# The head of an FNet-gated kernel: one chain of statistics, chunk 0 by pass, sums ahead of the second chunk's split, and the next operands written into the order

## The chip, the cores and the metric

The kernel runs on one core of a Trainium2 chip. The metric is device time in microseconds (us) of one execution, and the program has to fit one launch. Engines are named as in the profile: PE is TensorE (matmul), PEld its weight loads, DVE is VectorE, ACT is ScalarE, POOL is GpSimd, SP is SyncE, which issues most DMAs. "SPq" is SP's instruction queue.

## The reference, cut to what matters

Input x is [1, 2048, 512] in float32. The seq matrices are 2048 x 2048, the hidden ones 512 x 512, the layer between has 1792 units.

```python
xn = (x - mean(x)) / sqrt(var(x) + 1e-5)              # per row
a, b = xn @ dft_hid_re.T, xn @ dft_hid_im.T
s = dft_seq_re @ a - dft_seq_im @ b                   # real part of a 2-D DFT
h = relu(xn @ w1 + b1) ** 2
g = silu(h @ w2 + b2)
out = x + s * g
```

## The kernel before, in words

Every product in float32 is made of three matmuls: an operand is split into a high part (a copy rounded to the matmul's own format, written by ACT, `split_hi`, L70) and a low part (the remainder, a subtraction on DVE, `split_lo`, L73), and `PASSES` (L34) lists the three pairs high-high, high-low, low-high. The sequence transform comes first: chunks of 256 output rows (`c`, eight of them) by tiles of 2 x 128 input rows (`j`, eight of them). Chunks 0 and 1 are plain products; chunks 2 to 7 use a Strassen-like form with seven products (`mm`, L300, `PRODUCTS`, L50) on operands that `moving` (L217) makes: three sums on DVE (`sums_b`), then the splits into `g0` and `g1`. Then `stage2` (L282) multiplies a chunk's result, split into high and low parts (`pq`, L276, `pq_parts`, L169), with the hidden matrices (24 matmuls to a half, into one PSUM bank), ACT copies the bank to `ysb` (L295) and SP stores it to DRAM (`y`, L297). The layer with w1 and w2 and the gating follow; the change doesn't touch them.

The first part, L364 to L445, is a manual schedule: every engine's queue gets the instructions in the order in which the code writes them.

- *Start.* SP loads x and the constants `r` (of `ct`), tile 0 in halves: x one, r one, x two, r two. `WARM` (L21) gives 8 matmuls in bfloat16 and 5 in the other format on zeros. Tile 0 goes by halves: statistics (`ln_stats`, bn_stats and bn_aggr), root on ACT (`ln_root`), four small DVE operations (`ln_rstd`), `ln_xn`, splits, twelve matmuls, then the same for the second half.
- *Chunk 0.* For each tile `products` (L350) makes 24 matmuls of 128 x 512, two halves of twelve. By pass (tiles 0 to 3) all four blocks `k` go through high-high, then high-low, then low-high. Otherwise (tiles 4 to 7) each block makes its three matmuls in a row. The statistics of the next tile stand between the splits of this one.
- *Chunk 1.* Tile j's products need the constants' split of tile j, which `split(*plain_parts(1, j + 1))` (L434) makes one tile ahead into two buffers (`g1a`, `g1b`), so that it waits until the products of tile j - 1 are done. Beside the products, DVE and ACT work through a list `aside` (L426): the sums over xn (`sums`, L157) and their splits (`split_sums`, L179) for the operands of chunks 2 to 7, the splits of chunk 0's result (`pq_parts`), the hidden matrix's load and split (`wd_split`, L259). The loop takes items until their costs reach `ASIDE` = 4.2. `split_s1` (L184) follows one tile behind. `stage2(0, 0)` stands behind tile 6 and `stage2(0, 1)` behind tile 7.
- *Behind it.* `split_s1(7)`, `pq_parts(1)`. Then, outside the manual schedule, `prep()` (L649), which keeps up to three constant tiles loading and makes the operand of the next step, is called twice (L656) and once in each step of the loop at L659. There a scheduler places the instructions: it may put them ahead of what the manual schedule wrote last, on each engine's queue. The matmuls of that loop are issued after `plain_end`, the last matmul of `stage2(0, 1)`.

Tile pools tie the parts together: `r` has three buffers, `g1a` and `g1b` are those of the plain splits too, and `t` is shared by the sums over xn and by `moving`.

Of the kernel before, what the change touches and what calls it, by code (L numbers as in the profile page):

```python
# [16 lines left out]
NJ, NP = NS // 2, NF // 2  # L17
CW = 256
NC = S // CW
TC = 512  # L20
NTC = S // TC  # L21
WARM = 8, 5
PLAIN = 2

ASIDE = 4.2
# [8 lines left out]
PASSES = ((HI, HI), (HI, LO), (LO, HI))  # L34
# [30 lines left out]
def fnet_gated_kernel(ctx, tc, x, xt, ct, wd, w1, w2, b1, b2, out):  # L65
# [4 lines left out]
    def split_hi(hi, lo, src):  # L70
        nc.scalar.activation(hi, src, AF.Copy)  # L71

    def split_lo(hi, lo, src):  # L73
        return nc.vector.tensor_tensor(lo, src, hi.bitcast(F32), op=ALU.subtract)  # L74
# [37 lines left out]
    def load_x(j, hs=slice(0, 2)):  # L112

        if j not in xr:
            xr[j] = buf(f"pq{j // 2 % 2}{j % 2}", [P, 2, D], f"x{j}")
        nc.sync.dma_start(xr[j][:, hs], x.rearrange("(h j p) d -> j p h d", h=2, p=P)[j][:, hs])

    def ln_stats(j, hs=slice(0, 2)):
        t = xr[j]
        sm = buf("bn", [P, 12], f"bn{j}_{hs.start}", bufs=3)  # L120
        for h in range(hs.start, hs.stop):
            bn = sm[:, 6 * h:6 * h + 6]
            nc.vector.bn_stats(bn, t[:, h])
            nc.vector.bn_aggr(stats[:, :, h, j], bn)
# [3 lines left out]
    def ln_root(j, hs=slice(0, 2)):  # L128
        n = hs.stop - hs.start
        t = root[j] = buf("sm", [P, 4], f"root{j}_{hs.start}", bufs=3)  # L130
        nc.scalar.activation(t[:, 0:n], stats[:, 1, hs, j], AF.Sqrt, bias=eps)

    def ln_rstd(j, hs=slice(0, 2)):
        n = hs.stop - hs.start
        y, q = root[j][:, 0:n], root[j][:, 2:2 + n]
        var = rstd = stats[:, 1, hs, j]
        nc.vector.reciprocal(y, y)

        nc.vector.scalar_tensor_tensor(q, var, EPS, y, op0=ALU.add, op1=ALU.mult)
        nc.vector.scalar_tensor_tensor(q, q, -0.5, y, op0=ALU.mult, op1=ALU.mult)  # L140
        nc.vector.scalar_tensor_tensor(rstd, q, 1.5, y, op0=ALU.add, op1=ALU.mult)
# [9 lines left out]
    def xc_parts(j, h):  # L151
        s = slice(2 * h, 2 * h + 2)
        return XC[j][:, s, HI, :], XC[j][:, s, LO, :], halves(xn32[j][:, h])
# [30 lines left out]
    def split_s1(j):  # L184
        split(XC[j][:, S1, HI, :], XC[j][:, S1, LO, :], s1[j // ND][:, j % ND])
        return 0.4

    raw, part = {}, {}

    def load_c(c, j, hs=slice(0, 2)):  # L190
        if (c, j) not in raw:
            raw[c, j] = buf("r", [P, 4, CW], f"r{c}_{j}", bufs=3)
        q = slice(2 * hs.start, 2 * hs.stop)
        nc.sync.dma_start(raw[c, j][:, q], ct[c, j, :, q])

    def plain_parts(c, j, hs=slice(0, 2)):
        if (c, j) not in part:
            part[c, j] = buf("g1" + "ab"[j % 2], [P, 2, 4, CW], f"g{c}_{j}", F32R)
        g, r = part[c, j], raw[c, j]
        s = slice(2 * hs.start, 2 * hs.stop)  # L200
        return g[:, HI, s], g[:, LO, s], r[:, s]
# [15 lines left out]
    def moving(key, r):  # L217

        k = "ab"[turn[0] % 2]
        turn[0] += 1  # L220
        g0 = buf(f"g0{k}", [P, 2, 3, CW], f"g0_{key}", F32R)
        g1 = buf(f"g1{k}", [P, 2, 4, CW], f"g1_{key}", F32R)
        t = buf("t", [P, 4, CW], f"t_{key}", bufs=2)
        sums_b(t, r)
        split(g0[:, HI], g0[:, LO], r[:, I11:I21 + 1])
        split(g1[:, HI], g1[:, LO], t)
        return g0, g1
# [114 lines left out]
    def plain_banks(c):  # L342
        if c == 0:
            two_, b_, c_ = (bank(tag, f"pq0_{tag}") for tag in ("b2", "bb", "bc"))
            accs[c] = [two_[:, 0], two_[:, 1], b_[:, 0], c_[:, 0]]
        else:
            three_, a_ = (bank(tag, f"pq1_{tag}") for tag in ("b3", "ba"))
            accs[c] = [three_[:, 0], three_[:, 1], three_[:, 2], a_[:, 0]]

    def products(c, j, h, by_pass=False):  # L350

        g = part[c, j]
        for passes in [[q] for q in PASSES] if by_pass else [PASSES]:
            for k in range(ND):
                for a_, b_ in passes:
                    w = XC[j][:, 2 * h + k // 2, a_, k % 2 * P:(k % 2 + 1) * P]
                    nc.tensor.matmul(accs[c][k], w, g[:, b_, 2 * h:2 * h + 2],  # L357
                                     start=j == 0 and h == 0 and (a_, b_) == (HI, HI),
                                     stop=j == NJ - 1 and h == 1 and (a_, b_) == (LO, HI))

    one, two = slice(0, 1), slice(1, 2)
    order = [(c, j) for c in range(PLAIN) for j in range(NJ)]

    with tc.manual_schedule(engines=None):  # L364
        nc.scalar.activation(stats[:, 1, 0, 0:1], eps, AF.Sqrt)
        for hs in (one, two):
            load_x(0, hs)
            load_c(0, 0, hs)
        for j in range(1, 3):
            load_x(j)  # L370
            load_c(0, j)
        load_x(3)

        warm = bank("b3", "warm")[:, 0]
        for n, (count, dtype) in enumerate(zip(WARM, (mybir.dt.bfloat16, F32R))):
            zeros = buf("g0" + "ab"[n], [P, 512], f"zeros{n}", dtype)
            nc.vector.memset(zeros if n == 0 else zeros.bitcast(F32), 0.0)
            for _ in range(count):
                nc.tensor.matmul(warm, zeros[:, 0:P], zeros, start=True, stop=True)
        plain_banks(0)  # L380
        ln_stats(0, one)
        ln_root(0, one)
        for h, hs in enumerate((one, two)):
            g = plain_parts(0, 0, hs)
            split_hi(*g)
            ln_rstd(0, hs)
            ln_xn(0, h)
            split_hi(*xc_parts(0, h))
            if h == 0:
                ln_stats(0, two)  # L390
                ln_root(0, two)
            split_lo(*g)
            if h == 1:
                ln_stats(1)
                g = plain_parts(0, 1)
                split_hi(*g)
                ln_root(1)
            split_lo(*xc_parts(0, h))
            products(0, 0, h, True)
        load_c(0, 3)  # L400
        load_x(4)
        for j in range(1, NJ):
            ln_rstd(j)
            for h in range(2):
                ln_xn(j, h)
                split_hi(*xc_parts(j, h))
            split_lo(*g)
            load_c(*order[j + 3])
            if j + 4 < NJ:
                load_x(j + 4)  # L410
            split_lo(*xc_parts(j, 0))
            if j + 1 < NJ:
                ln_stats(j + 1)
                ln_root(j + 1)
            split_lo(*xc_parts(j, 1))
            for h in range(2):
                products(0, j, h, j < 4)
            g = plain_parts(*order[j + 1])
            split_hi(*g)
            if j == 2:  # L420
                nc.sync.dma_start(b1s, b1)
                nc.sync.dma_start(b2s, bcast(b2, D))
        split_lo(*g)


        aside = chain(sums(0), (split_sums(j) for j in range(ND)), pq_parts(0), wd_split(0),  # L426
                      sums(1), (split_sums(j) for j in range(ND, NJ)), wd_split(1))
        plain_banks(1)
        for j in range(NJ):
            n = NJ + j  # L430
            if n + 3 < len(order):
                load_c(*order[n + 3])
            if j + 1 < NJ:
                split(*plain_parts(1, j + 1))  # L434
            for h in range(2):
                products(1, j, h)
            spent = 0
            if j:
                spent = split_s1(j - 1)
            while spent < ASIDE:  # L440
                spent += next(aside, ASIDE)
            if j > NJ - 3:
                plain_end = stage2(0, j - NJ + 2)
        split_s1(NJ - 1)
        list(pq_parts(1))  # L445
    raw.clear()


    W1, W2, H, fin = {}, {}, {}, {}
# [188 lines left out]
    def plus(c, e, k, cols=slice(0, 2)):  # L638
# [1 line left out]
        z = e[:, k, w]  # L640
        nc.vector.tensor_tensor(z, z, fin[c][2 + k // 2][:, k % 2, w], op=ALU.add)
        nc.sync.dma_start(at(out[c * TC:(c + 1) * TC], k)[:, cols], z.rearrange("p (k e) -> p k e", e=256))

    steps = [(c, j) for c in range(PLAIN, NC) for j in range(NJ)]
    AHEAD = 2
    todo = list(steps)
    loads = list(steps)

    def prep():  # L649
        while loads and len(raw) < 3:  # L650
            load_c(*loads.pop(0))
        if todo:
            s = todo.pop(0)
            part[s] = moving(f"{s[0]}_{s[1]}", raw.pop(s))

    for j in range(AHEAD):  # L656
        prep()

    for c, j in steps:  # L659
        if j == 0:  # L660
            ms = banks(c)
        g = part.pop((c, j))
# [261 lines left out]
```

## Time and profile before

| what | us |
|---|---|
| median of the runs (717.65 to 718.12) | 717.79 |
| the profiled execution's own time | 717.76 |
| its span, first to last instruction | 716.0 |
| TensorE busy | 706.6 |
| first product of chunk 0, tile 0 | 7.16 |
| first product of chunk 0, tile 1 | 14.45 |
| first product of chunk 1 | 55.10 |
| first matmul of stage2(0, 1) | 106.39 |
| first product of chunk 2 | 111.99 |

A row of the timeline has the start, the duration, the engine, the line and operation, what is written and read, how many were merged, and in brackets how long the engine stood idle before it and what ended that. A row of the windows has, for a stretch of the span, each engine's busy time and count, then the granted TensorE clock, the DMA share and GB/s. Matmuls are pipelined: a row's duration has the drain in it, so that the step from one start to the next is what a matmul costs. Times are from the span's start.

### The profile page before, as it was taken

What the parts mean: (1) busy time and instruction counts of PE and PEld (TensorE: products, weight loads), DVE (VectorE), ACT (ScalarE), POOL (GpSimd) and SP (SyncE); (2) the same over time, 40 slices, a digit from 0 to 9 for tenths busy, and PEclk for the clock granted to TensorE, in tenths of its full rate; (3) what the DMA queues carried; (4) which work ended last, traced back from release to release, by engine and by line L of the source; (5) the groups of instructions that cost most, each with busy time, mean ns of one, the idle gap of its engine ahead of it and who ended that gap; (6) DMA issues with size and microseconds to landing.
All of it is one profiled execution on the core that took longest, in us unless ns stands there. A gap on an engine that the chain in (4) does not pass through costs nothing.

```text
span 716.0 us, 12693 instructions
## 1 busy us (share of the span) xinstructions
PE 706.6 (99%) x5149; PEld 665.4 (93%) x5149; DVE 585.2 (82%) x887; ACT 348.2 (49%) x475; POOL 5.2 (1%) x8
## 2 busy tenths in 40 slices
PE   8999999999999999999999999999999999999996
PEld 5778778999999999999998999999999999999996
DVE  7987964679599697797796864999988989989897
ACT  4434533444453444544443423767767774444451
POOL 0000000000000000000000000000000000101000
PEclk9999999999999999999999999999999999999999
DMA  8524340623563553743833678975733996676644
GB/s 287 198 102 162 121 162 16 221 99 138 194 219 133 206 192 133 255 172 120 289 122 113 230 276 295 355 282 195 269 120 148 350 406 215 187 224 163 221 143 152
DMA packets 55018, 141.09 MB, mean 197 GB/s; under 512 B 5040, under 2 KB 21680, under 8 KB 53680
## 3 DMA queue, kind: packets, MB, share of 16 engines
q1 hardware_dynamic: 49840, 124.56, 50.0%
q10 hardware_dynamic: 4032, 14.68, 5.2%
q0 software_dynamic: 1088, 1.05, 1.0%
q8 instruction: 40, 0.66, 0.4%
q14 instruction: 18, 0.15, 0.1%
HBM read 97.00 MB, written 43.27 MB: 196 GB/s over the span
## 4 chain that ended last, share of the span: by engine, by line
PE 92%; DVE 5%; DMA 1%; issue 1%; ACT 0%; DVEq 0%; SPq 0%
PE m_b L304 24%; PE yps L289 13%; PE m_b_o L591 10%; PE hps L537 10%; PE hps_b L537 6%; PE m_bb L304 5%; PE m_ba L304 5%; PE pq_b L357 5%; PE m L591 3%; PE hps_ba L537 3%; PE m_bb_o L591 2%; PE m_ba_o L591 1%; PE m_bc_o L591 1%; PE hps_bb L537 1%; DVE g L74 1%; PE pq_ba L357 1%
## 5 line engine op out<-in xcount | busy, mean ns | idle before, releaser
L304 PE MATMUL m_b<-g,xc 128*128 128x256 f32 x1440 | 181.3, 281 | 0.0
L304 PEld LDWEIGHTS m_b<-g,xc 128*128 128x128 f32 x1440 | 175.5, 189 | 0.4
L74 DVE TENSOR_TENSOR g<-r,g 128x768 fp32r<-128x768 f32 (+2 forms) x65 | 65.5, 1008 | 54.8 <-ACT g L71 54.8
L71 ACT ACTIVATE g<-r 128x768 fp32r<-128x768 f32 (+2 forms) x65 | 57.7, 888 | 95.5 <-PE m_b L304 52.2
L289 PE MATMUL yps<-wd,pq 128*128 128x512 f32 x384 | 93.8, 395 | 0.0
L289 PEld LDWEIGHTS yps<-wd,pq 128*128 128x128 f32 x384 | 70.4, 188 | 15.3
L591 PE MATMUL m_b_o<-w,g 128*128 128x256 f32 x588 | 75.2, 283 | 0.0
L591 PEld LDWEIGHTS m_b_o<-w,g 128*128 128x128 f32 x588 | 72.3, 191 | 0.1
L357 PE MATMUL pq_b<-g,xc 128*128 128x512 f32 x240 | 65.3, 400 | 2.5 <-ACT xc L71 1.3
L74 DVE TENSOR_TENSOR g<-t,g 128x1024 fp32r<-128x1024 f32 x48 | 58.7, 1222 | 8.8 <-ACT g L71 8.7
L537 PE MATMUL hps<-xT,w 128*128 128x256 f32 x504 | 61.9, 282 | 0.0
L537 PEld LDWEIGHTS hps<-xT,w 128*128 128x128 f32 x504 | 60.9, 190 | 0.1
L357 PEld LDWEIGHTS pq_b<-g,xc 128*128 128x128 f32 x240 | 44.0, 188 | 16.7 <-ACT xc L71 3.3
L71 ACT ACTIVATE g<-t 128x1024 fp32r<-128x1024 f32 x48 | 50.3, 1048 | 14.4 <-PE m_ba L304 6.8
L548 ACT ACTIVATE h<-h,b1s 128x512 f32<-128x512 f32 x56 | 37.4, 716 | 17.6 <-DVE h L254 17.6
L71 ACT ACTIVATE g<-hr 128x768 fp32r<-128x768 f32 (+1 forms) x28 | 35.5, 1266 | 21.1 <-DVE hr L213 5.3
L74 DVE TENSOR_TENSOR g<-hr,g 128x768 fp32r<-128x768 f32 (+1 forms) x28 | 41.6, 1485 | 2.3 <-ACT g L71 2.2
L304 PE MATMUL m_bb<-g,xc 128*128 128x256 f32 x288 | 43.3, 283 | 0.0
L304 PE MATMUL m_ba<-g,xc 128*128 128x256 f32 x288 | 42.9, 281 | 0.0
L304 PEld LDWEIGHTS m_bb<-g,xc 128*128 128x128 f32 x288 | 39.3, 189 | 1.8
L304 PEld LDWEIGHTS m_ba<-g,xc 128*128 128x128 f32 x288 | 38.0, 189 | 0.0
L537 PE MATMUL hps_b<-xT,w 128*128 128x256 f32 x288 | 36.2, 282 | 0.0
(167 smaller groups left out, 1018.7 us busy)
## 6 DMA issues: line engine op xcount, KB each, us to landing
r<-in_ct SPq DMA_DIRECT2D x63, 512.0 KB, 3.6
hd<-h ACTq DMA_DIRECT2D x28, 512.0 KB, 4.2
hr<-hd SPq DMA_DIRECT2D x28, 512.0 KB, 4.2
w1d<-w0g SPq DMA_DIRECT2D x21, 512.0 KB, 3.2
w<-w1d SPq DMA_DIRECT2D x6, 1792.0 KB, 9.7
w<-w2d SPq DMA_DIRECT2D x4, 1792.0 KB, 9.9
y<-ysb SPq DMA_DIRECT2D x16, 256.0 KB, 3.1
fin<-y SPq DMA_DIRECT2D x16, 256.0 KB, 5.1
```

The lines of the kernel that those rows point to most:

```text
L71: nc.scalar.activation(hi, src, AF.Copy)
L74: return nc.vector.tensor_tensor(lo, src, hi.bitcast(F32), op=ALU.subtract)
L289: ins = nc.tensor.matmul(ps, PQ[c, m, k // 2][:, a_, w:w + P], WD[m, k][:, b_, :], start=n == 0, stop=n == 2 * ND * 3 - 1)
L304: nc.tensor.matmul(ps[:, d * CW:(d + 1) * CW], w[:, a_, d * P:(d + 1) * P], mv(b_), start=first and d == 0 and (a_, b_) == (HI, HI), stop= ...
L357: nc.tensor.matmul(accs[c][k], w, g[:, b_, 2 * h:2 * h + 2], start=j == 0 and h == 0 and (a_, b_) == (HI, HI), stop=j == NJ - 1 and h == 1 ...
L537: nc.tensor.matmul(product(ms, k), W1[p][a][:, a_, q * P:(q + 1) * P], xT[c, q][:, b_, b], start=share not in first, stop=q == 1 and (a_, ...
L548: nc.scalar.activation(x_[:, s], x_[:, s], AF.Relu, bias=b1s[:, f:f + 1])
L591: nc.tensor.matmul(m[:, k * 256:(k + 1) * 256], g[:, a_, a, k * P:(k + 1) * P], W2[p][:, b_, b], start=p == 0 and k == 0 and (a_, b_) == ( ...
```

## The change

- `WARM` gets 8 instead of 5 of the second kind of warm-up matmul.
- SP loads both halves of x's tile 0 before both halves of the constants.
- Tile 0 has one chain of statistics for both halves (operations on 128 x 2 instead of twice 128 x 1). On DVE both `ln_xn` come next, then the low parts of both constant halves, the low part of xn's first half, the statistics of tile 1, the low part of the second half. Both halves' matmuls follow.
- All of chunk 0 goes by pass, tiles 4 to 7 too.
- `beside(0)` takes from `aside` once before chunk 1's loop, so that the four sums over xn stand ahead of the split of (1, 1), and each later item one tile earlier.
- `prep()` is moved into the manual schedule: the first call stands behind the loop of chunk 1 and so behind `stage2(0, 1)` with its copy and its store, the second behind `pq_parts(1)`. Its loads stand where it is called.

```diff
-WARM = 8, 5
+WARM = 8, 8
...
-        for passes in [[q] for q in PASSES] if by_pass else [PASSES]:
+        for passes in [PASSES] if c else [[q] for q in PASSES]:
...
+    def prep():
+        while loads and len(raw) < 3:
+            load_c(*loads.pop(0))
+        if todo:
+            s = todo.pop(0)
+            part[s] = moving(f"{s[0]}_{s[1]}", raw.pop(s))
...
         for hs in (one, two):
             load_x(0, hs)
+        for hs in (one, two):
             load_c(0, 0, hs)
...
-        ln_stats(0, one)
-        ln_root(0, one)
+        ln_stats(0)
+        ln_root(0)
+        split_hi(*plain_parts(0, 0, one))
+        ln_rstd(0)
         for h, hs in enumerate((one, two)):
-            g = plain_parts(0, 0, hs)
-            split_hi(*g)
-            ln_rstd(0, hs)
             ln_xn(0, h)
             split_hi(*xc_parts(0, h))
             if h == 0:
-                ln_stats(0, two)
-                ln_root(0, two)
-            split_lo(*g)
-            if h == 1:
-                ln_stats(1)
-                g = plain_parts(0, 1)
-                split_hi(*g)
-                ln_root(1)
-            split_lo(*xc_parts(0, h))
-            products(0, 0, h, True)
+                split_hi(*plain_parts(0, 0, two))
+        for hs in (one, two):
+            split_lo(*plain_parts(0, 0, hs))
+        split_lo(*xc_parts(0, 0))
+        ln_stats(1)
+        g = plain_parts(0, 1)
+        split_hi(*g)
+        ln_root(1)
+        split_lo(*xc_parts(0, 1))
+        for h in range(2):
+            products(0, 0, h)
...
+        def beside(spent):
+            while spent < ASIDE:
+                spent += next(aside, ASIDE)
+
+        beside(0)
         for j in range(NJ):
...
-            spent = 0
-            if j:
-                spent = split_s1(j - 1)
-            while spent < ASIDE:
-                spent += next(aside, ASIDE)
+            beside(split_s1(j - 1) if j else 0)
             if j > NJ - 3:
                 plain_end = stage2(0, j - NJ + 2)
+        raw.clear()
+        prep()
         split_s1(NJ - 1)
         list(pq_parts(1))
-    raw.clear()
+        prep()
...
-    for j in range(AHEAD):
-        prep()
```

More of the change, by code (lines that the diff above doesn't have):

```diff
@@ L348, in plain_banks, with products @@
             accs[c] = [three_[:, 0], three_[:, 1], three_[:, 2], a_[:, 0]]
-    def products(c, j, h, by_pass=False):
+    def products(c, j, h):
         g = part[c, j]
-        for passes in [[q] for q in PASSES] if by_pass else [PASSES]:
+        for passes in [PASSES] if c else [[q] for q in PASSES]:
             for k in range(ND):
@@ L362, in fnet_gated_kernel @@
     order = [(c, j) for c in range(PLAIN) for j in range(NJ)]
+    steps = [(c, j) for c in range(PLAIN, NC) for j in range(NJ)]
+    todo = list(steps)
+    loads = list(steps)
+    def prep():
[4 more added lines that the diff above has]
+            part[s] = moving(f"{s[0]}_{s[1]}", raw.pop(s))
     with tc.manual_schedule(engines=None):
@@ L416, in fnet_gated_kernel @@
             for h in range(2):
-                products(0, j, h, j < 4)
+                products(0, j, h)
             g = plain_parts(*order[j + 1])
@@ L642, in plus @@
         nc.sync.dma_start(at(out[c * TC:(c + 1) * TC], k)[:, cols], z.rearrange("p (k e) -> p k e", e=256))
[L644 to L654, printed above, removed]
-    for j in range(AHEAD):
-        prep()
     for c, j in steps:
```

## The prediction, made before the changed kernel ran

> **What bounds the kernel now.** Read first the chain of waits and the DMA issues on the page, then the windows that cut the span at the chunks, then the timeline engine by engine where a window shows idle TensorE.
>
> ```profile
> PE 92%; DVE 5%; DMA 1%; issue 1%; ACT 0%; DVEq 0%; SPq 0%
> ...
> r<-in_ct SPq DMA_DIRECT2D x63, 512.0 KB, 3.6
> ```
>
> ```profile
> 106.40:424.00 317.60, 317.60 (x2374) 303.29 (x2373) 245.24 (x363) 136.46 (x186) 0.00 (x0) 1.00 0.50 174
> 424.00:710.00 286.00, 285.99 (x2355) 283.60 (x2354) 248.82 (x347) 163.17 (x209) 4.99 (x4) 1.00 0.67 233
> ```
>
> From 106.4 to 710 us TensorE (first busy figure of each window) has no idle time. So the end is the start of that dense stretch plus a fixed amount of matmul work: what the change does before 106.4 moves the end one for one, and a hole opened at the head of the dense stretch does so too. The change touches only that part; past the first tiles of chunk 2 the built program of the changed kernel has the same instructions in the same order.
>
> **Part 1, start and chunk 0.**
>
> ```profile
> 3.77 0.69 DVE L123 BATCH_NORM_STATS2 bn<-x 128x6 f32<-128x512 f32 x1 [2.06 <-DMA x<-in_x]
> 4.57 0.18 DVE L124 BATCH_NORM_AGGREGATE stats<-bn 128x2 f32<-128x6 f32 x1
> ...
> 6.48 0.63 ACT L71 ACTIVATE xc<-xn 128x512 fp32r<-128x512 f32 x1 [0.87 <-DVE xn L148]
> ...
> 7.16 0.73 PE L357 MATMUL pq_b<-g,xc 128*128 128x512 f32 x2 [0.40 <-ACT xc L71]
> ...
> 8.05 0.64 ACT L71 ACTIVATE g<-r 128x512 fp32r<-128x512 f32 x1 [0.46 <-DMA r<-in_ct]
> ...
> 10.21 0.69 DVE L123 BATCH_NORM_STATS2 bn<-x 128x6 f32<-128x512 f32 x1
> ...
> 11.83 0.66 DVE L74 TENSOR_TENSOR xc<-xn,xc 128x512 fp32r<-128x512 f32 x1
> ...
> 12.40 0.16 DVE L137 RECIPROCAL root<-root 128x2 f32<-128x2 f32 x1
> ...
> 14.45 0.74 PE L357 MATMUL pq_b<-g,xc 128*128 128x512 f32 x2 [0.73 <-ACT xc L71]
> ```
>
> One chain of statistics for both halves puts a second pair of bn_stats and bn_aggr (0.8 us, the step from 3.77 to 4.57) ahead of the first root: first product at 7.95 instead of 7.16. The second half of x, now second on SP, has 0.9 us behind the first for its 256 KB; were it late, the first product would be, but tile 1's chain hangs on a later landing: the second constant half lands fourth in either order (8.03), ScalarE has it split at 8.69, then come on VectorE its low part, the low part of xn and the two statistics of tile 1: 8.72 + 0.6 + 0.6 gives 9.91 for bn_stats instead of 10.21. The 1.62 us from there to the low part at 11.83 and the 2.62 us to the product at 14.45 stay. Tile 1 starts 0.30 us earlier, at 14.15. Four small operations and a root that go stood beside that landing and bring nothing. Bounds: no gain, or 0.8 if that half lands earlier; I take 0.3. The three added warm-up matmuls end before 7.95, as the clock is full from about 6.4; at worst they cost 0.1.
>
> ```profile
> 31.42 0.43 PE L357 MATMUL pq_b<-g,xc 128*128 128x512 f32 x1
> 32.27 1.81 PE L357 MATMUL pq_b<-g,xc 128*128 128x512 f32 x5 [0.42 <-DVE g L74]
> ...
> 55.10 2.26 PE L357 MATMUL pq_b<-g,xc 128*128 128x512 f32 x9
> ```
>
> ```profile
> 46.20 0.16 DVE L137 RECIPROCAL root<-root 128x2 f32<-128x2 f32 x1
> ```
>
> By pass in tiles 4 to 7: a product takes 0.233 us (24 in 5.6 us). At tile 4 the second product needs the low part of the constants, so it starts 0.85 us after the first instead of 0.23, and five take 1.81 us instead of 1.33. With a 0.1 at tile 7 that makes 1.2 us. By pass the low part is needed after four products, 0.93 us in, and tile 4's release (32.27) came 0.85 in: just in time. VectorE sets the pace from there: the reciprocals of tiles 1 and 7, at 12.40 and 46.20, are six tiles of 5.63 us apart against TensorE's 5.60, which takes 0.05 back. So chunk 1 begins at 55.10 - 0.30 - 1.15 = 53.65.
>
> **Part 2, chunk 1.** The four sums over xn now come before the second constant tile's split.
>
> ```profile
> 50.72 1.23 DVE L74 TENSOR_TENSOR g<-r,g 128x1024 fp32r<-128x1024 f32 x1 [0.30 <-ACT g L71]
> 56.40 1.23 DVE L74 TENSOR_TENSOR g<-r,g 128x1024 fp32r<-128x1024 f32 x1 [4.45 <-ACT g L71]
> 57.54 1.22 DVE L166 TENSOR_TENSOR s<-xn 128x1024 f32<-128x1024 f32 x1
> ...
> 88.44 1.22 DVE L74 TENSOR_TENSOR g<-r,g 128x1024 fp32r<-128x1024 f32 x1
> ```
>
> ```profile
> 88.70 0.39 PE L357 MATMUL pq_b<-g,xc 128*128 128x512 f32 x1
> 89.71 2.13 PE L357 MATMUL pq_b<-g,xc 128*128 128x512 f32 x8 [0.62 <-DVE g L74]
> ```
>
> Before, VectorE idles 4.45 us and then falls behind: the low part for tile 6 is late and costs 0.9 us (1.01 for a step of 0.23, and 0.1 refilling). Afterwards the sums fill the idle time, from 51.2, but all later side work comes one tile earlier too. From the first sum to that low part VectorE spent 57.54 to 88.44 = 30.9 us. The new list between the two has one more constant split (1.14), one more xn split (0.87) and four splits of wd (2.4) in it, and lacks two sums of the next operand (1.3 with their wait): 34.0 if the waits for ScalarE stay as they are, some 36.3 if the pairs of pq, the xn splits behind the last sum and the wd splits behind the last xn split each wait as such pairs wait before. So the low part starts between 85.2 and 87.5; TensorE needs it to start by 86.2 (53.65 + 6 x 5.6 + 0.23 - 1.27). Loss between 0 and 1.4 us; I take 1.4, as nearly all of these splits wait for ScalarE before. Against the old 0.9 the gain of 1.45 shrinks to 0.9: chunk 1 with both its stage 2 pieces ends at 111.1 instead of 111.99.
>
> **Part 3, the next operands.** Before, prep() stood outside the written order, and the rows show its loads and splits early, in the middle of chunk 1.
>
> ```profile
> 95.64 5.70 SPq L194 DMA_DIRECT2D r<-in_ct  x2
> 101.61 11.53 SPq L297 DMA_DIRECT2D y<-ysb  x2
> ```
>
> ```profile
> 106.39 5.76 PE L289 MATMUL yps<-wd,pq 128*128 128x512 f32 x24
> 106.63 1.06 ACT L71 ACTIVATE g<-t 128x1024 fp32r<-128x1024 f32 x1 [4.75 <-issue]
> 107.72 1.23 DVE L74 TENSOR_TENSOR g<-t,g 128x1024 fp32r<-128x1024 f32 x1 [5.38 <-ACT g L71]
> 108.98 0.69 DVE L205 TENSOR_TENSOR t<-r 128x512 f32<-128x512 f32 x1
> ...
> 110.17 0.42 DVE L207 TENSOR_TENSOR t<-t,r 128x256 f32<-128x256 f32 x1
> 111.99 0.88 PE L304 MATMUL m_bb<-g,xc 128*128 128x256 f32 x6
> 112.18 0.60 ACT L295 ACTIVATE ysb<-yps 128x512 f32<-128x512 f32 x1 [4.49 <-PE yps L289]
> ```
>
> Now the first prep() stands behind stage2(0, 1) in the written order. Its three loads of constants stand on SP behind both y stores, the second of which waits for ScalarE's copy of the very PSUM bank that TensorE finishes last; on ScalarE its split stands behind that copy. In the built program's SP list the order is y, y, then r of (2, 0), (2, 1), (2, 2), and TensorE's next instruction after stage 2 is the product of (2, 0). So:
>
> - last stage 2 product at 111.1; copy 0.19 later for 0.60: 111.9; the y store issued at once (112.78 to 112.81 before), the load 0.4 behind it: 112.3;
> - landing 3.6 us later by the page's DMA issues: 115.9;
> - on ScalarE the high part of g0, 0.85: TensorE's first product at about 116.8;
> - on VectorE three sums, 1.61 (108.98 to 110.59), then the low part of g0, 0.96: the third product at 118.5.
>
> TensorE stands from 111.1 to 118.5 but for two products of 0.12: 7.2 us.
>
> ```profile
> 113.46 0.42 DVE L74 TENSOR_TENSOR pq<-pq_b,pq 128x256 fp32r<-128x256 f32 x1
> ...
> 118.48 0.41 DVE L74 TENSOR_TENSOR pq<-pq_ba,pq 128x256 fp32r<-128x256 f32 x1
> 124.15 0.96 DVE L74 TENSOR_TENSOR g<-r,g 128x768 fp32r<-128x768 f32 x1 [5.26 <-ACT g L71]
> ...
> 126.11 0.85 ACT L71 ACTIVATE g<-r 128x768 fp32r<-128x768 f32 x1 [1.00 <-PE m_b L304]
> ```
>
> ```profile
> DMA to landing us min/median/max: 3.2/5.0/9.2
> ```
>
> Behind the splits of g1 (1.06 and 1.23) come the eight pq splits, which hand over between ScalarE and VectorE pair by pair: 5.4 us for eight before with three sums between them, some 4.7 without, so from 120.1 to 124.8. In the built program TensorE runs stage2(1, 0) inside tile (2, 0) and reaches its second block of pq at 121.6, while ScalarE has its high part at 122.9: 1.2 us more. The operand of tile (2, 1) is complete by 129.8, when TensorE still has that work. Together 8.4 us. Bounds: a landing of 3.2 to 5.0 us (the fastest and the median load of r in the crowded first 30 us, the last row), no wait or 2 us for pq: 6.8 to 10.6.
>
> **The clock.**
>
> ```profile
> 1.22 5.54 PE L379 MATMUL warm<-zeros 128*128 128x512 bf16 x13 [1.22 <-DVE zeros L377]
> ```
>
> ```profile
> 712.00:713.00 1.00, 0.00 (x0) 0.00 (x0) 0.94 (x2) 0.00 (x0) 0.00 (x0) 0.99 0.38 131
> 713.00:714.00 1.00, 0.00 (x0) 0.00 (x0) 0.00 (x0) 0.00 (x0) 0.00 (x0) 0.50 0.47 167
> ```
>
> The granted clock falls to half 2.9 us after the last product (710.1). At the start the warm-up matmuls run 0.43 us apart, the products from 7.16 on 0.23: full speed came some 5.2 us after 1.22. Here TensorE stands 7 us, so it resumes at half clock. If that holds for 5.2 us, to 123.7, it costs up to 2.6 us of work, of which the 1.2 us wait for pq hides its share: 1.4. Bounds 0 and 1.4; I take 0.9, as the fall is seen to come well inside such a stand and the rise is seen once only. The Trainium skill, "TensorE: Matmul & The Clock Gate", Part 1, says that half clock returns after an idle window of about 3.4 us, and full clock after one busy window of that length. An estimate by that figure has half clock to 121.9 and would make this term 0.5; the trace's fall agrees, its rise took longer.
>
> **The sum.** -0.9 (parts 1 and 2) + 8.4 + 0.9 = +8.4 us on the profiled execution's 717.76 (span 716.0 and 1.76 around it; the median of the runs is 717.79): 726.2 us. The hole is only at this place: later preps find their loads issued a tile or more ahead.
>
> **Rivals.**
>
> *The load isn't held.* If the stores' wait didn't hold what stands behind it on SP, as the change would then not put the loads where it writes them, only ScalarE's queue would bind: copy to 111.9, high part to 112.75, low part to 113.7, 2.4 us, with pq 1.2 more, and no fall of the clock: 717.76 - 0.9 + 3.6 = 720.5. Against it: between the issues from 101.61 to 113.14 SP issued nothing else, and the built list is in this order. The Trainium skill, "DMA: Bandwidth & Descriptors", Anatomy of one DMA, says that a semaphore wait is held on the issuing sequencer before dispatch, which speaks against this rival as well; no load stood behind a waiting store in this trace, so that it can't show it.
>
> *Faster.* VectorE's relief wins: chunk 0 ends 1.45 us earlier, chunk 1 loses nothing, and the new operand is ready in time. That needs a load issued by 104.9 (3.6 + 1.6 + 0.96 ahead of 111.1), and ScalarE's split ahead of its copy: then 717.76 - 1.45 - 0.9 = 715.4. With the loss in chunk 1 kept it is 716.9, within the bound of no change. For it: VectorE's 4.45 us of idle time is real. Against it: both queues' order.
>
> **How the numbers follow.** Held load 0.88: 726.2, between 723.4 (-2.35 + 8.0: chunk 1 loses nothing, fast landing, no fall of the clock) and 728.9 (-0.9 + 10.6 + 1.4). Load not held 0.06: 720.5. Faster 0.03: 715.4; no change 0.03: 716.9. The range 723.0 to 728.9 leaves the rivals out with little over 1 in 10. A change under 0.2% (1.4 us) can't be told from none; so faster 0.03, same 0.03, slower 0.94.
>
> **What would show it.** Right: the first product near 7.95, tile 1 near 14.15, chunk 1 from about 53.65; SP issuing the load of (2, 0) only after the second y store, near 112.3; a stand of TensorE near 111 to 118.5 put down to ScalarE's or VectorE's g, behind a DMA of r; a granted clock below 1 near 115 to 124; then dense to the end. Wrong: a load of r issued before 105, or TensorE dense across 111.

## The result and the profile after

| what, us | before | predicted | changed |
|---|---|---|---|
| median of the runs (changed: 724.80 to 727.27) | 717.79 | 726.2 | 725.37 |
| the profiled execution's own time | 717.76 | | 727.27 |
| first product of chunk 0, tile 0 | 7.16 | 7.95 | 7.70 |
| first product of chunk 0, tile 1 | 14.45 | 14.15 | 13.65 |
| first product of chunk 1 | 55.10 | 53.65 | 53.11 |
| end of stage2(0, 1), counted at 0.233 a matmul | 111.99 | 111.1 | 109.53 |
| first product of chunk 2 | 111.99 | 116.8 | 115.38 |
| third product of chunk 2 | | 118.5 | 117.02 |

The ratio is 1.0106, 95% interval 1.009 to 1.0123: about 1% slower. The profiled execution was the longest of its five runs; the last part of this section says why.

**The hole.** These are waits of TensorE in the changed kernel, with total, number of times and longest:

```profile
PE m_bb L304 <- ACT g L71: 5.7, 1, 5.7
PE hps_ba L553 <- DMA w1b<-w1d: 1.1, 1, 1.1
...
PE m_bb L304 <- DVE g L74: 0.8, 1, 0.8
PE m_b_o L607 <- ACT m_b_o L600: 0.8, 2, 0.5
```

The first and third of these belong to the first product of chunk 2. The timeline there, all engines, rows in order of their start:

```profile
105.79 3.90 PE L289 MATMUL yps<-wd,pq 128*128 128x512 f32 x16
...
109.73 0.60 ACT L295 ACTIVATE ysb<-yps 128x512 f32<-128x512 f32 x1 [10.30 <-PE yps L289]
110.35 0.33 SPq L297 DMA_DIRECT2D y<-ysb  x1
110.73 6.59 SPq L194 DMA_DIRECT2D r<-in_ct  x4
114.48 0.84 ACT L71 ACTIVATE g<-r 128x768 fp32r<-128x768 f32 x1 [4.16 <-DMA r<-in_ct]
114.48 0.69 DVE L205 TENSOR_TENSOR t<-r 128x512 f32<-128x512 f32 x1 [14.60 <-DMA r<-in_ct]
...
115.38 0.58 PE L304 MATMUL m_bb<-g,xc 128*128 128x256 f32 x1 [5.69 <-ACT g L71]
...
116.01 0.95 DVE L74 TENSOR_TENSOR g<-r,g 128x768 fp32r<-128x768 f32 x1
...
117.02 1.44 PE L304 MATMUL m_bb<-g,xc 128*128 128x256 f32 x5 [0.84 <-DVE g L74]
...
122.11 0.38 ACT L71 ACTIVATE pq<-pq_ba 128x256 fp32r<-128x256 f32 x1
...
122.27 0.30 PEld L289 LDWEIGHTS yps<-wd,pq 128*128 128x128 f32 x2 [0.40 <-ACT pq L71]
```

Read it as a relay: TensorE ends stage 2, ACT copies the bank, SP issues the y store and only then the loads of r, the first of them lands, ACT makes the high part of g0 and DVE, idle for 14.60 us, three sums and the low part. The wait that the summary writes to "ACT g" is thus a DMA, which is a store's place in SP's queue. SP alone:

```profile
99.15 11.53 SPq L297 DMA_DIRECT2D y<-ysb  x2
110.73 1.41 SPq L194 DMA_DIRECT2D r<-in_ct  x3
```

Between the first y store at 99.15 and the second SP issues nothing; then the three loads go out one after the other. The Trainium skill, "DMA: Bandwidth & Descriptors", Anatomy of one DMA (a section on DMAs that GpSimd issues), says that a semaphore wait is held on the issuing sequencer before dispatch. The trace of before couldn't show it; this one agrees for SP: the loads come 0.38 us after the store that waited for ACT's copy. The windows of 2 us (behind the length TensorE's busy time; behind the five engines granted clock, DMA share, GB/s) show the stand and the clock:

```profile
110.00:112.00 2.00, 0.00 (x0) 0.00 (x0) 0.00 (x0) 0.32 (x1) 0.00 (x0) 1.00 0.42 143
112.00:114.00 2.00, 0.00 (x0) 0.00 (x0) 0.00 (x0) 0.00 (x0) 0.00 (x0) 1.00 0.92 313
114.00:116.00 2.00, 0.62 (x2) 0.50 (x2) 1.45 (x3) 0.84 (x1) 0.00 (x0) 0.52 1.04 397
116.00:118.00 2.00, 1.16 (x5) 0.98 (x5) 1.69 (x3) 1.63 (x3) 0.00 (x0) 0.50 0.18 66
118.00:120.00 2.00, 2.00 (x11) 1.90 (x10) 1.55 (x4) 0.38 (x1) 0.00 (x0) 0.50 0.71 260
120.00:122.00 2.00, 2.00 (x11) 1.68 (x9) 0.90 (x3) 0.94 (x3) 0.00 (x0) 0.77 0.03 8
```

A stand of 7.49 us less two products of 0.12, from 109.53 to 117.02, then, until 122.6, half clock and the handovers of pq between ACT and DVE: 9.29 us over what the same matmuls take at full speed without waits.

**Ahead of the hole** 2.46 us were gained (stage2(0, 1) starts at 103.93, not 106.39): 0.80 up to tile 1, 1.19 in chunk 0 (39.46 from tile 1 to chunk 1, 40.65 before), 0.47 in chunk 1, where tile 5 now loses 0.36 and tile 6 only 0.05 (0.9 before). DVE and PE there:

```profile
80.33 1.22 DVE L74 TENSOR_TENSOR g<-r,g 128x1024 fp32r<-128x1024 f32 x1
...
85.97 1.23 DVE L74 TENSOR_TENSOR g<-r,g 128x1024 fp32r<-128x1024 f32 x1
```

```profile
81.11 2.62 PE L357 MATMUL pq_b<-g,xc 128*128 128x512 f32 x9
...
87.07 2.31 PE L357 MATMUL pq_b<-g,xc 128*128 128x512 f32 x9
```

The group that starts tile 5 takes 2.62 instead of 2.26 us, since its low part ends at 81.55; that of tile 6, 2.31. Before, tile 6's low part started at 88.44, now at 85.97.

**Behind it** the profiled execution has something that nobody forecast:

```profile
467.27 0.88 PE L553 MATMUL hps_ba<-xT,w1a 128*128 128x256 f32 x6
469.24 0.98 PE L553 MATMUL hps_ba<-xT,w1b 128*128 128x256 f32 x6 [1.10 <-DMA w1b<-w1d]
...
614.05 1.70 PE L607 MATMUL m_b_o<-w,g 128*128 128x256 f32 x12 [0.48 <-ACT m_b_o L600]
...
616.76 1.46 PE L607 MATMUL m_b_o<-w,g 128*128 128x256 f32 x10 [0.30 <-ACT m_b_o L600]
```

A load of w1b lands after it is needed, and two copies on ACT are late. These waits are most of the 2.68 us that are lost behind the hole. So this execution is -2.46 + 9.29 + 2.68 = +9.51, which is 727.27 less 717.76. The profile of the same kernel in run e12 below has no wait for w1b, and its sum is -2.34 + 9.34 + 0.27 = +7.27 (725.04 less 717.76: +7.28). Such waits are not the change's own: the traces of e2, e3 and e11 below wait 0.4, 1.1 and 0.3 us for w1b too, and e11 is the kernel before with other preparations. That the runs of the changed kernel between 724.8 and 725.85 have a part of them is argued, not shown.

### The profile page after: what moved, and what is told of

It reads as the page before. It is cut to its first block, busy times and chain, and to the rows that moved or that the text cites. A ratio compares the mean times of both kernels' runs of the same rounds, so it can differ in the third digit from the quotient of the medians.

```text
span 725.5 us, 12697 instructions
## 1 busy us (share of the span) xinstructions
PE 709.0 (98%) x5152; PEld 666.9 (92%) x5152; DVE 585.1 (81%) x883; ACT 347.3 (48%) x474; POOL 5.2 (1%) x8
## 4 chain that ended last, share of the span: by engine, by line
PE 90%; DMA 4%; DVE 4%; ACT 1%; issue 1%; SPq 0%; DVEq 0%; ACTq 0%
PE m_b L304 24%; PE yps L289 12%; PE m_b_o L607 10%; PE hps L553 8%; PE pq_b L357 6%; PE m_bb L304 5%; PE hps_b L553 5%; PE m_ba L304 5%; DMA w1b<-w1d 3%; PE m L607 3%; PE hps_ba L553 2%; PE m_bb_o L607 2%; PE pq_bc L357 1%; PE pq_bb L357 1%; PE m_ba_o L607 1%; PE m_bc_o L607 1%
## 5 line engine op out<-in xcount | busy, mean ns | idle before, releaser
L71 ACT ACTIVATE g<-r 128x768 fp32r<-128x768 f32 (+2 forms) x65 | 57.6, 887 | 90.8 <-PE m_b L304 50.2
L357 PE MATMUL pq_b<-g,xc 128*128 128x512 f32 x240 | 67.1, 398 | 1.2 <-ACT xc L71 1.0
L71 ACT ACTIVATE g<-t 128x1024 fp32r<-128x1024 f32 x48 | 50.3, 1047 | 12.3 <-PE m_ba L304 6.8
L71 ACT ACTIVATE g<-hr 128x768 fp32r<-128x768 f32 (+1 forms) x28 | 35.5, 1266 | 21.1 <-DVE hr L213 5.3
L205 DVE TENSOR_TENSOR t<-r 128x512 f32<-128x512 f32 x48 | 32.8, 686 | 14.8 <-DMA r<-in_ct 14.6
```

The source lines that it names most:

```text
L205: nc.vector.tensor_tensor(t[:, 0:2], r[:, 0:1].to_broadcast([P, 2, 256]), r[:, 1:3], op=ALU.add)
L357: nc.tensor.matmul(accs[c][k], w, g[:, b_, 2 * h:2 * h + 2], start=j == 0 and h == 0 and (a_, b_) == (HI, HI), stop=j == NJ - 1 and h == 1 ...
```

## The experiments

Three groups of runs, each on one chip with the kernel before beside it (its median: 717.74 for e1 to e3 and e8, 717.88 for e4 to e7, 718.45 for e9 to e12). The ratios go by these. The first theory was the prediction's: held loads make the hole, DVE's volume makes the loss in chunk 1.

**e1, the changed kernel with both preparations back outside the written order.**

```diff
-        raw.clear()
-        prep()
         split_s1(NJ - 1)
         list(pq_parts(1))
-        prep()
+    raw.clear()
+    prep()
+    prep()
```

> The changed kernel with both prep() calls back outside the written order; start, by pass and sums stay changed. Theory (the hole at the head of chunk 2 comes from the written place of prep, the rest of the change gains): no hole, dense TensorE across the end of stage2(0, 1), about 715.3 (717.8 less the 2.5 us by which stage2(0, 1) starts earlier in the changed kernel's trace, 103.93 against 106.39), up to 716.3 if the next operands' sums in the middle of chunk 1 bring its stall back. Rival (the loss comes from the new start or from the sums' place, which leave VectorE behind): stays above 722.

718.49 us, ratio 1.001 (1.0001 to 1.0019): a miss. There is no hole at chunk 2, as expected, but a new one in chunk 1. TensorE and DVE there:

```profile
87.10 0.39 PE L357 MATMUL pq_b<-g,xc 128*128 128x512 f32 x1
90.06 2.40 PE L357 MATMUL pq_b<-g,xc 128*128 128x512 f32 x7 [2.58 <-DVE g L74]
```

```profile
86.64 0.69 DVE L205 TENSOR_TENSOR t<-r 128x512 f32<-128x512 f32 x1 [1.88 <-DMA r<-in_ct]
...
88.79 1.22 DVE L74 TENSOR_TENSOR g<-r,g 128x1024 fp32r<-128x1024 f32 x1
```

L205 is a sum of the preparation for tile (2, 0). Outside the written order the scheduler puts it on DVE ahead of tile 6's split, and DVE stands 1.88 us until its load lands. The split follows at 88.79, the products stand 2.7 us and half clock comes on top (91.20 to 94.61, see the last section). Before's stall of 0.9 us at tile 6 is in part of this kind too: its sum waited 0.39 us for the same load. The time of the two sums that stand ahead of the split (L205 and L206, 0.61 and 0.33 from start to start) is the larger part.

```profile
85.76 0.69 DVE L205 TENSOR_TENSOR t<-r 128x512 f32<-128x512 f32 x1 [0.39 <-DMA r<-in_ct]
```

The load is issued as soon as tile 5's split frees its buffer (before: 80.81 + 1.22 = 82.03, issue 82.05; e1: 80.35 + 1.22 = 81.57, issue 81.59). It lands at 85.74 and 86.62, so that it took 3.69 us before and 5.03 in e1; why it took longer stays open. The second theory was made of this: *a preparation at a written place takes the sum, and the stall with it, out of chunk 1; behind the store it opens the hole.* Its rival remained DVE's volume.

**e2, the kernel before with only the preparations moved** as in the change.

> The kernel before with only prep moved to its written place behind stage2(0, 1) and pq_parts(1). Theory: a hole of about 9.3 us as in the changed kernel, less up to 0.9 for the stall of chunk 1 that the moved sums may remove: 726.2 to 727.1. Rival (the hole needs the earlier start of the rest, or the cost is spread): under 721.

725.81 us, ratio 1.0109 (1.0095 to 1.0123), 0.4 us under the theory's range and far from the rival's: a hole of 9.15 us and no loss at tile 6. This part alone gives the whole slowdown.

**e3, the changed kernel with the loads of chunk 2's first tiles early**, in chunk 1's loop.

```diff
-            if n + 3 < len(order):
-                load_c(*order[n + 3])
+            load_c(*(order + steps)[n + 3])
...
-        raw.clear()
+        for k in order:
+            raw.pop(k, None)
+        del loads[:3]
         prep()
```

> The changed kernel with the loads of (2, 0), (2, 1), (2, 2) written in the loop of chunk 1 like all loads before them, so that they stand ahead of the second y store on SP; prep's sums and splits stay where they are. Theory (the load held behind the y store is most of the hole, ScalarE's queue the rest): the hole shrinks to some 3.6 us (copy, high part and low part in 2.4, pq handovers 1.2), so about 719 to 719.7. Rival 1 (only SP's order counts): 715.3. Rival 2 (only ScalarE's order counts): no gain, 725.

719.51 us, ratio 1.0023 (1.0014 to 1.0031), as expected. The load is there long before; now ACT's queue binds, the high part (L71) standing behind the copy (L295):

```profile
109.75 0.60 ACT L295 ACTIVATE ysb<-yps 128x512 f32<-128x512 f32 x1 [10.30 <-PE yps L289]
110.24 0.83 ACT L71 ACTIVATE g<-r 128x768 fp32r<-128x768 f32 x1
...
111.11 0.96 DVE L74 TENSOR_TENSOR g<-r,g 128x768 fp32r<-128x768 f32 x1 [9.68 <-ACT g L71]
...
112.12 1.44 PE L304 MATMUL m_bb<-g,xc 128*128 128x256 f32 x5 [0.49 <-DVE g L74]
```

The hole is 4.05 us. So of 9.3 us the load behind the store is 5.2, and ACT's place behind the copy, with the handovers of pq and half clock, the rest.

**e4, the changed kernel with 22 idle matmuls in the hole** (nothing reads their result), to keep the clock up.

```diff
+        warm2 = bank("bb", "warm2")[:, 0]
+        for _ in range(22):
+            nc.tensor.matmul(warm2, XC[0][:, 0, HI, 0:P], XC[0][:, 0:2, HI, :], start=True, stop=True)
         raw.clear()
         prep()
```

> The changed kernel with 22 matmuls of 128 x 512 behind stage2(0, 1) whose result nothing reads (5.1 us, inside the 5.9 us for which TensorE stands), so that the clock has no idle window. Theory as on record (half clock costs 0.9 us): about 724.5. Theory after reading the trace (the half clock lies beside the wait for the pq splits, which ends at 122.3 to 122.6 either way): 725.2 to 725.4, no gain that can be told. Rival (the clock is the larger part of the hole): under 723.

725.27 us, ratio 1.0103 (1.0087 to 1.0118): no gain that can be told. The prediction's price of half clock, 0.9 us, would have given 724.5. TensorE behind the hole:

```profile
122.57 1.67 PE L289 MATMUL yps<-wd,pq 128*128 128x512 f32 x6 [0.17 <-ACT pq L71]
```

Half clock lasts 3.4 us (117.67 to 121.08) instead of 6.8 (114.08 to 120.91), yet the hole is 9.44 us: TensorE waits for ACT's pq at 122.57 as the changed kernel does at 122.27. This tests less than it seems. Most of the half clock that went lay in the stand: TensorE works at half clock for 3.4 us here and, but for two products, for 3.9 in the changed kernel (117.02 to 120.91). That a full clock would gain nothing is read from the waits: in both traces TensorE is through with its slow work before ACT's high part of pq is there, so a faster TensorE would wait longer for it. No run had the clock full across the hole.

**e5, e6, e7, the kernel before with one part alone:** the new start; `products(0, j, h, True)` for all of chunk 0; `beside(0)` ahead of the loop.

> The kernel before with only the new start: loads of x first, one chain of statistics, eight warm-up matmuls. Theory: tile 1 starts at 13.65 as in the changed kernel's trace instead of 14.45 and all behind it follows: 0.8 us faster, 717.0. Rival (the first product half a microsecond later counts): 718.3. Theory on record had 0.3 to 0.8.

717.73 us, ratio 1.0001 (0.9992 to 1.001): a miss. Tile 1 starts at 13.67, but tile 6 stands 1.52 us:

```profile
85.72 0.69 DVE L205 TENSOR_TENSOR t<-r 128x512 f32<-128x512 f32 x1 [1.13 <-DMA r<-in_ct]
```

DVE comes to the sum 0.78 us earlier than before (84.59 against 85.37), and the load is issued 0.78 earlier (81.27), but it takes 4.42 us instead of 3.69 and lands at the same time. The wait grows by 0.74 us, and TensorE's loss at tile 6 by the same (0.78 before the refilling, now 1.52): the wait holds the split one for one, and the gain is lost again.

> The kernel before with only tiles 4 to 7 of chunk 0 by pass. Theory: the stall at tile 4 goes, 1.2 us, and what VectorE does in chunk 1 starts as much earlier since it waits for the end of chunk 0: 716.6. Rival (chunk 1's stall grows by what chunk 0 gains, since VectorE is the bound there): 717.8.

716.60 us, ratio 0.9983 (0.9974 to 0.9991): as expected. By pass is worth 1.2 to 1.3 us. Here DVE and the load both come earlier by about as much, and the sum waits 0.49 us, little more than before.

> The kernel before with only the sums over xn ahead of the split of (1, 1). Theory: VectorE's 4.45 us of idle time are used, the stall of 0.9 us at tile 6 goes or falls to a few tenths: 717.0 to 717.3. Rival (side work one tile earlier makes other splits late, as the prediction had it): 717.8 or slower.

717.98 us, ratio 1.0003 (0.9994 to 1.0012): a miss, and the time that the rival named. The sum waits 0.67 us and the stall is 1.15:

```profile
86.34 0.69 DVE L205 TENSOR_TENSOR t<-r 128x512 f32<-128x512 f32 x1 [0.67 <-DMA r<-in_ct]
```

It comes about in the rival's way: behind the earlier side work tile 5's split runs at 81.25 instead of 80.81, and with it the load is issued (82.50) and lands (86.32) later.

**e8, the changed kernel with early loads (e3's) and both preparations behind the products of tile (1, 7), ahead of stage2(0, 1).**

```diff
             beside(split_s1(j - 1) if j else 0)
+            if j == NJ - 1:
+                for k in order:
+                    raw.pop(k, None)
+                del loads[:3]
+                prep()
+                prep()
             if j > NJ - 3:
                 plain_end = stage2(0, j - NJ + 2)
-        raw.clear()
-        prep()
         split_s1(NJ - 1)
         list(pq_parts(1))
-        prep()
```

> The changed kernel with the loads early as in the other run and both prep() calls written behind the products of (1, 7), ahead of stage2(0, 1), so that neither SP's store nor ScalarE's copy stands before them. Theory: no hole and no stall by the next operands, dense from chunk 1 on: 715.0 to 715.5, faster than both kernels. Rival (written order is worse than the scheduler's at any place, since the splits of g1 of (2, 1) wait for the products of (1, 7) and hold up the copy of stage 2): above 717.

715.59 us, ratio 0.9966 (0.9952 to 0.9979), faster than both kernels and 0.1 us above the expected range. No hole: the splits run beside tile 7's products, and chunk 2 follows stage 2 at once.

```profile
99.39 0.84 ACT L71 ACTIVATE g<-r 128x768 fp32r<-128x768 f32 x1
...
103.99 5.76 PE L289 MATMUL yps<-wd,pq 128*128 128x512 f32 x24
...
109.59 0.87 PE L304 MATMUL m_bb<-g,xc 128*128 128x256 f32 x6
```

**e9, e8 without the sums ahead** (`beside(0)` left out).

> As the kernel with the loads early and both preparations behind products (1,7), which took 715.59 us, but without the sums over xn ahead of the split of tile (1,1). Theory (the stall of tile 6 of chunk 1 comes from the preparation's sum, which waits for a load on VectorE; with the preparations at a written place the sums' place is worth little): 715.6 to 716.5 us, no stall of over 0.5 us at tile 6. Rival (VectorE's volume in chunk 1 makes the stall, and the sums ahead take it out): the stall of about 0.9 us is back, 716.5 us or more.

715.44 us, ratio 0.9962 (0.995 to 0.9975), a little under the theory's range. DVE's idle time is back, and TensorE loses nothing, in tile 5 either:

```profile
54.59 1.22 DVE L74 TENSOR_TENSOR g<-r,g 128x1024 fp32r<-128x1024 f32 x1 [3.68 <-ACT g L71]
...
79.01 1.22 DVE L74 TENSOR_TENSOR g<-r,g 128x1024 fp32r<-128x1024 f32 x1
```

So the idle time cost nothing. With the sums ahead, in e8, tile 5's split runs at 80.41 and its products take 2.61 us instead of 2.26, while here it runs at 79.01. The volume rival as it was put falls. What goes with the preparation's place is both the sum's wait and the sums' own 0.94 us, and no run parts these two in before's 0.9.

**e10, e8 with the old start.**

> As the kernel that took 715.59 us, but with the old start (first products at 7.2 us, tile 1 at about 14.45 instead of 13.65). Theory (the start is worth 0.8 us once nothing in chunk 1 waits for a load): 716.1 to 716.4 us. Rival (the start is worth nothing, as in the run of the start alone): 715.6 us.

716.21 us, ratio 0.9974 (0.9962 to 0.9985): 0.6 us above e8 (715.59) and 0.8 above e9 (715.44). It is the theory's number, but the intervals of the ratios overlap, and ahead of chunk 2 the traces show 0.36 us of it (first product 109.95, in e8 109.59); e10's trace also has a late copy near 605 us, 0.38 us, that has nothing to do with the start. So once nothing in chunk 1 waits for a load, the start pays, by some 0.4 us.

**e11, the kernel before with e8's loads and preparations alone.**

> The kernel before with only the loads of tiles (2,0) to (2,2) early and both preparations behind products (1,7), ahead of the second stage of tile (0,1). Theory (the preparation's sum is what stalls tile 6 of chunk 1): the stall of 0.9 us goes, no hole at chunk 2, 716.9 us. Rival (VectorE's volume stalls it): the stall stays, 717.8 us.

717.10 us, ratio 0.9985 (0.9976 to 0.9994), near the theory. The start, chunk 0 and the sums are those of before, and the stall at tile 6 is gone: its split starts 1.8 us earlier than before's 88.44 (0.4 of it because the whole chunk starts earlier, 54.71 against 55.10), without a sum of the preparation ahead of it.

```profile
86.63 1.22 DVE L74 TENSOR_TENSOR g<-r,g 128x1024 fp32r<-128x1024 f32 x1
```

```profile
88.31 2.26 PE L357 MATMUL pq_b<-g,xc 128*128 128x512 f32 x9
```

**e12, the changed kernel again.**

> The changed kernel itself, for another profile. Theory (the waits for the load of w1b near 468 us and for the bias copies near 614 us, 2.7 us together in its first profile, come in some executions only): the hole of about 9.3 us near 112 us is there, the late waits are smaller or gone, and the time of the profiled execution is then near 725 us; median 725.0 to 725.5 us. Rival (they belong to the kernel): the same waits of 2.7 us, and a profiled execution near 727 us.

725.40 us, ratio 1.0101 (1.0087 to 1.0115). The hole is there (5.8 us of wait for g, 9.34 in all); the w1b matmuls follow without a wait:

```profile
467.44 0.88 PE L553 MATMUL hps_ba<-xT,w1a 128*128 128x256 f32 x6
468.16 0.87 PE L553 MATMUL hps_ba<-xT,w1b 128*128 128x256 f32 x6
```

The late waits come in some executions only. Where w1b's time goes in the others (it landed at 469.20 there, at 467.06 here) stays open.

## Why the prediction was right, and where it was wrong

- *Start, 0.30 gained:* 0.80 in this pair of profiles, the upper bound it gave. It put the second constant half's landing at 8.03 in either load order; in the changed kernel it landed at 6.40. But the profile before is a late one: in the five other traces with the old order that half landed at 6.64 to 7.20, and tile 1 started at 14.05 to 14.28, not 14.45. With the new start it started at 13.65 to 13.82 in eight traces. The means are 0.44 apart, so that the predicted 0.30 is nearer than the 0.80.
- *Chunk 0 by pass, 1.2 (1.15 net):* 1.19 in the trace, 1.2 to 1.3 in e6. Right.
- *Chunk 1, a loss of 1.4 against 0.9 before:* this step failed. The low part of tile 6 began at 85.97, inside the predicted 85.2 to 87.5, near its early end, and what was lost is 0.41, nearly all of it at tile 5. The cause was misread as well: the prediction charged the 0.9 to DVE falling behind after 4.45 us of idleness. It did count the preparation's two sums as 1.3 us that go. It did not see that these stand ahead of the split and that the first waits there for a load (e1, e5), that the written place of the preparation is what removes the stall (e11), and that the idle time costs nothing (e9).
- *Parts 1 and 2 together, 0.9:* 2.46, from these two terms; all times of part 3 come 1.57 us earlier for it.
- *The hole, 8.4:* right step by step. With this shift the forecast is: copy done 110.3, load 110.7, landing 114.3, first product 115.2, third 116.9; measured 110.33, 110.73, 114.46, 115.38, 117.02. Until there it is 7.25 (predicted 7.2).
- *Wait for pq 1.2, clock 0.9:* the sum is right (2.04 measured), the division isn't, and that the sum came out is partly luck. The two lie beside each other and don't add: TensorE works at half clock until 120.91 and still waits for pq, whose handovers end the hole at 122.3 to 122.6. So pq alone is worth 2.0, and by this wait the clock nothing more (e4 bears it out for 0.5 us of slow work only).
- *The total:* +8.4 predicted; +7.28 in e12's profile, +7.6 by the medians. The gain ahead of the hole was 1.5 larger, the hole 9.3 as the terms 8.4 and 0.9 say, and late waits give 0.3 to 2.7.
- *The rivals:* "the load isn't held" was priced 3.6 us with no fall of the clock; e3, where the load is issued early, makes 4.05, with a fall. Why "faster" did not happen: it asked for a load issued by 104.9 and for ACT's split ahead of its copy. e8 gives both, and takes 715.59 where the rival said 715.4.

## What to carry to other kernels

Before moving work to a written place, write down what then stands ahead of it on every in-order queue it uses: here one store's wait on SP and one copy on ACT cost 9.3 us, and the same code some lines earlier, with its loads early, cost nothing. Where an engine is late, look for the instruction in its queue that waits for a DMA before counting its volume. Work that gets faster ahead of such a wait gains only if the load comes sooner too: the wait was 0.39, 0.49, 0.67, 1.13 and 1.88 us in before, e6, e7, e5 and e1, in the order of the time from the load's issue to its landing (3.69, 3.78, 3.82, 4.42 and 5.03 us). Idle time of an engine ahead of a stall is no proof that filling it helps.

## What the runs showed of the hardware

The granted clock fell after shorter stands than the 2.9 us that the prediction had seen: in e1 after one of 2.6 us, at 91.20, when TensorE had been at work again for over 1 us; in e3 after waits of 1.4 and 0.5 us with two products between; in e4 after waits of 0.8 and 1.1 us behind the 22 matmuls. The changes of the granted clock, as the traces record them, show a pattern. Between two of them there is always a whole number of stretches of 3.413 us (25 of them in e1 up to the fall, 31 in e3, 32 in the changed kernel). The first rise comes anywhere from 4.85 to 6.99 us in the fourteen traces, though the warm-up starts at 1.22 in all of them. So the clock changes on a grid of 3.413 us that does not start with the kernel. These are the grid's windows ahead of the falls in e1, e3 and e4, and one in e5 that left the clock full:

```profile
87.79:91.20 3.41, 1.14 (x5) 0.97 (x6) 3.41 (x7) 0.95 (x2) 0.00 (x0) 1.00 0.44 150
...
108.68:112.09 3.41, 1.53 (x7) 0.79 (x5) 0.98 (x2) 2.34 (x4) 0.00 (x0) 1.00 0.20 77
...
114.26:117.67 3.41, 1.45 (x8) 0.83 (x7) 2.50 (x5) 2.02 (x3) 0.00 (x0) 1.00 0.67 269
...
88.49:91.90 3.41, 2.23 (x10) 1.81 (x11) 3.41 (x5) 1.04 (x2) 0.00 (x0) 1.00 0.34 125
```

TensorE was busy for 1.14, 1.53 and 1.45 us ahead of the falls, and for 2.23 us where the clock stayed. Over all windows at full clock in the fourteen traces, those with up to 1.54 us of work were followed by half clock and those with 1.56 us or more were not. So what counted here is TensorE's busy share of such a window, with a limit near 45% (TensorE's ends are modelled, so that the second digit is not sure), and not the length of one stand. At half clock, windows with up to 1.77 us kept it, and windows with 3.38 us or more ended it. Between matmuls, half clock lasted one window (3.4 us) in e1, e3 and e4 and two (6.8 us) in the changed kernel, e2 and e12. The Trainium skill, "TensorE: Matmul & The Clock Gate", Part 1, has half clock after an idle window of about 3.4 us. The length of the windows agrees; that the window be idle was not needed here.
